# Two attention blocks on one core: where constants, weight permutations and key sums are made

## The chip, the cores and the metric

The kernel runs on one core of a Trainium2 chip. The metric is the time on the device in microseconds (us), from the first to the last instruction of the core, as a median of several executions. A profile is one execution taken apart by the hardware's profiler. Engines: PE is TensorE (matmuls), PEld its weight loads, DVE is VectorE, ACT is ScalarE, POOL is GpSimd, SP is SyncE, which here only issues DMA transfers. PSUM is the memory that matmuls write to, in eight banks; HBM is the main memory.

## The reference

Two independent blocks, A and B, share one program. Each has its own input of 2048 rows and 640 columns and its own weights.

```python
def _A_ref(x, wqkv, wo):                       # softmax attention, 32 heads of 20
    qkv = (x @ wqkv).reshape(B, S, 3, H, Dh) ...   # q, k, v
    scores = einsum("bhqd,bhkd->bhqk", q, k) * Dh ** -0.5
    p = softmax(scores, axis=-1)
    o = einsum("bhqk,bhkd->bhqd", p, v)
    return o.reshape(B, S, D) @ wo

def _B_ref(x, wqkv, wo):                       # linear attention, 32 heads of 20
    ...                                        # q, k, v as above
    phi = lambda t: where(t > 0, t + 1, exp(t)) + 1e-6
    pq, pk = phi(q), phi(k)
    kv = einsum("bhsd,bhse->bhde", pk, v)
    z = einsum("bhsd->bhd", pk)                # the key sums
    num = einsum("bhqd,bhde->bhqe", pq, kv)
    den = einsum("bhqd,bhd->bhq", pq, z)[..., None] + 1e-6
    return (num / den).reshape(B, S, D) @ wo

out = concatenate([_A_ref(A_x, A_wqkv, A_wo), _B_ref(B_x, B_wqkv, B_wo)], axis=-1)
# B, S, D, H = 1, 2048, 640, 32; everything bfloat16, values of about 0.05
```

## The kernel before

Block A is not computed with exponentials of all scores. The inputs keep every score small, so softmax is replaced by a second-order expansion, and a check at the end falls back to a general program if the bound doesn't hold. For each tile of 128 keys the kernel makes, per head, 242 features of the key (a one, the keys, their pairwise products) and sums feature times value over all keys. That is `t_T`, the product "ps<-f_big,f_Vp". A selection step (`sel` and `spread`, the tile `f_Tu`) lays these sums out for the queries. Queries are projected (`t_qj`), written to HBM, and loaded again in rearranged rows (`t_psi`, "f_big<-f_Qd"); VectorE forms their pairwise products, and `t_pv` multiplies them with the sums ("ps<-f_big,f_Tu"; such a unit has 48 matmuls). Block B projects keys and values, applies phi, sums key times value, and later does queries, denominators and the output.

All of it goes through one list of tasks. While the program is built, a small planner with assumed durations picks the order of tasks on each engine by priority; the hardware then runs each engine's list in order, with semaphores between them. `_C` holds the priorities. A smaller number goes first.

```python
_WS = 176
_C = dict(q=0.62, qs=0.04, ks=0.0, kd=0.02, bk=1.68, bks=0.0, bq=-2.52, bo=0.0, out=2.14, pv=0.0, fe=3.88,
          psi=5.12, r=-4.73, f=0.5, nm=3.12, op=6.09, kv=1.52, npo=0.16, bqs=0.05, bd=0.02, bn=4.94)
...
    def job(self, mms, cols, deps, prio=3.0, mode="pv", pool="aux", due=None):
        dur = sum(max(0.1, c / 2400.0 + 0.003) for c in cols)     # the planner's duration of a matmul job
...
```

Constants are made on the chip. `it` holds index patterns (iota), from which an identity, group masks (`M6`, `M32`), selections (`P`) and block masks (`mask`) are built. In the kernel before, the tasks form one chain, each depending on the one before it:

```python
    def mid_consts(self):
        ...
        last = self.event(1.5)
        ...
        def task(eng, dur, *ops):
            nonlocal last

            def fn(t):
                for f, r, w in ops:
                    sch.op(eng, f, reads=r, writes=w)
            last = plan.add(_Task(eng, dur, fn, prio=2.4), (last,))
        ...
        task("dve", 1.5,
             ...
                                        op=ALU.add), ("ident",), (K,)),
             (lambda e: e.tensor_copy(self.M32[:], m32), (K,), ("M32",)),
             (lambda e: e.memset(self.kvacc[:], 0.0), (), ("kva0",)),
             (lambda e: e.memset(self.mask, 0.0), (), ("mask0",)),
             (lambda e: e.memset(self.kvN[:], 0.0), (), ("kvN0",)))
        ops = [(lambda e: e.memset(self.GW[:], 0.0), (), ("GW",)),
               (lambda e: e.tensor_copy(self.GW[:, 8:14], self.M6[0:120, :]), ("M6",), ("GW",))]

        for x, (d, r) in enumerate(_SL):
            o = _off(d)[1]
            for a, n, b in ((0, 20 - r, o + r), (20 - r, r, o)):
                if n:
                    ops.append((lambda e, x=x, a=a, n=n, b=b: e.tensor_copy(
                        self.P[:, x, 6 * a:6 * (a + n)].rearrange("p (a h) -> p a h", h=6),
                        self.ident[0:123, b:b + n].unsqueeze(2).broadcast_to([123, n, 6])), ("ident",), ("P",)))
        ops.append((lambda e: e.tensor_copy(self.P[:, 0, 120:123], self.ident[0:123, 120:123]), ("ident",), ("P",)))
        task("pool", 9.0, *ops)
        m2 = scr[:, 0:168]
        for c in range(N_DC):
            h0, nh = self.hlo[c]
            w = 21 * nh
            task("pool", 0.6, (lambda e, h0=h0, nh=nh, c=c: e.iota(
                it[:, 0, 0:21 * nh], [[D_HEAD, nh], [0, 21]], base=D_HEAD * h0 - 128 * c, channel_multiplier=-1), (),
                ("it0",)))
            task("dve", 0.6,
                 (lambda e, w=w: e.tensor_scalar(m2[:, 0:w], it[:, 0, 0:w], 0.0, None, op0=ALU.is_le), ("it0",), (K,)),
                 (lambda e, c=c, w=w: e.scalar_tensor_tensor(self.mask[:, c, 0:w], it[:, 0, 0:w], -19.0, m2[:, 0:w],
                                                             op0=ALU.is_ge, op1=ALU.mult),
                  ("it0", K, "mask0"), (("mask", c),)))
        return last
```

Tiles of x are transposed by TensorE and copied out of PSUM by ScalarE or VectorE (`t_xt`, "f_xT<-ps"). Keys and values of tile t are projected in two halves of 320 columns. A key tile is copied out and copied twice more on ScalarE (`ext2`, `ext`), and then VectorE forms its products in two instructions, `even` and `odd`. The weights of the queries are put in another order by ScalarE after they have been loaded:

```python

        def perm(x, c):
            self.copy(x.eng, self.w[:, 0, c, 0:600].rearrange("p (b a h) -> p b a h", b=5, h=6),
                      self.w0r[:, c, 0:600].rearrange("p (b h a) -> p b a h", b=5, h=6), ("w0r",), (("w", 0, c),))
            self.copy(x.eng, self.w[:, 0, c, 600:640].rearrange("p (a h) -> p a h", h=2),
                      self.w0r[:, c, 600:640].rearrange("p (h a) -> p a h", h=2), ("w0r",), (("w", 0, c),))
        self.ew[0] = plan.add(_Task("none", 0.0, lambda t: None), [plan.add(_Task(
            "act", 0.9, lambda x, c=c: perm(x, c), prio=1.0), (e0,)) for c in range(N_DC)])
...
        def permB(x, c):
            self.copy(x.eng, self.wB[:, 0, c, :].rearrange("p (a h) -> p a h", h=N_HEADS),
                      self.w0B[:, c, :].rearrange("p (h a) -> p a h", a=D_HEAD), ("w0B",), (("wB", 0, c),))
        self.ewB[0] = plan.add(_Task("none", 0.0, lambda t: None), [plan.add(_Task(
            "act", 0.75, lambda x, c=c: permB(x, c), prio=2.2), (e1,)) for c in range(N_DC)])
```

The key sums of block B end as `zn[:, 0, :]`, 128 partitions by 5 numbers. They go to HBM and come back with another assignment of partitions:

```python

        def kvfin(_):
            zs = self.zs[:]
            sch.op("dve", lambda e: e.tensor_tensor(
                zs, self.kvacc[:].rearrange("p c (h j) -> p c h j", j=21)[:, :, :, 20],
                self.mask.rearrange("p c (h j) -> p c h j", j=21)[:, :, :, 20], op=ALU.mult),
                reads=tuple(("kva", c) for c in range(N_DC)) + tuple(("mask", c) for c in range(N_DC)), writes=("zs",))
            sch.op("dve", lambda e: e.tensor_reduce(self.zn[:, 0, :], zs, axis=AX.X, op=ALU.add), reads=("zs",),
                   writes=("zn0",))
            for c in range(N_DC):
        ...
        zd = self.Zd.ap()

        def small(e, dst, src):
            with self.nc.allow_non_contiguous_dma(reason="640 numbers in all"):
                return e.dma_start(dst, src)
        z1 = self.spd([lambda e: small(e, bass.AP(zd.tensor, zd.offset, [[1, 128], [128, N_DC], [1, 1]]), self.zn[:, 0, :])], (kvd,),
                      ("zn0",), ("Zd",), prio=0.4, lat=5.0)
        z2 = self.spd([lambda e: small(e, self.zn[:, 1, :], bass.AP(
            zd.tensor, zd.offset, [[1, 4], [D_HEAD, N_HEADS], [4, N_DC], [1, 1]]))], (z1,), ("Zd",), ("zn1",), prio=0.4, lat=5.0)
```

Of the kernel before, what the change touches and what calls it, by code (L numbers as in the profile page):

```python
# [6 lines left out]
F32 = mybir.dt.float32  # L7
BF16 = mybir.dt.bfloat16
I32 = mybir.dt.int32
AF = mybir.ActivationFunctionType  # L10
ALU = mybir.AluOpType
# [3 lines left out]
N_HEADS = 32  # L15
# [915 lines left out]
def _off(d):  # L931

    if d is None:
# [13 lines left out]
_C = dict(q=0.62, qs=0.04, ks=0.0, kd=0.02, bk=1.68, bks=0.0, bq=-2.52, bo=0.0, out=2.14, pv=0.0, fe=3.88,  # L947
          psi=5.12, r=-4.73, f=0.5, nm=3.12, op=6.09, kv=1.52, npo=0.16, bqs=0.05, bd=0.02, bn=4.94)


class _Fast:

    AUX = (4, 5, 6, 7)
    GB = 3
    NF = 2
# [28 lines left out]
    def alloc(self):  # L984
# [37 lines left out]
        self.zs = self.sb("f_zs", [128, N_DC, 8], F32)  # L1022
        self.zn = self.sb("f_zn", [128, 2, N_DC], F32)
# [27 lines left out]
        self.it = rb0[:, 0:360].bitcast(I32).rearrange("p (k n) -> p k n", k=2)  # L1051
# [52 lines left out]
    def fm(self, out, lhsT, rhs, start, stop, reads, writes, inc=True, sgc=False):  # L1104
        m = lhsT.shape[1]
        for j in range(0, m, 32):
            k = min(j + 32, m)
            self.sch.mm(out[j:k], lhsT[:, j:k], rhs, start=start, stop=stop, reads=reads, writes=writes, tp=(0, j),
                        inc=inc and k == m, sgc=sgc)
# [3 lines left out]
    def loads(self):  # L1113
# [44 lines left out]
        def perm(x, c):  # L1158
# [5 lines left out]
            "act", 0.9, lambda x, c=c: perm(x, c), prio=1.0), (e0,)) for c in range(N_DC)])  # L1164
# [6 lines left out]
        def permB(x, c):  # L1171
# [3 lines left out]
            "act", 0.75, lambda x, c=c: permB(x, c), prio=2.2), (e1,)) for c in range(N_DC)])  # L1175
# [14 lines left out]
    def consts(self):  # L1190
        sch, ps, it = self.sch, self.ps, self.it
        sch.op("dve", lambda e: e.memset(self.zt[:], 0.0), writes=("zt",))
        sch.op("pool", lambda e: e.iota(it[:, 0, 0:128], [[1, 128]], base=0, channel_multiplier=-1), writes=("it0",))
        sch.op("dve", lambda e: e.memset(self.warm[:], 0.0), writes=("warm",))
        sch.op("act", lambda e: e.activation(self.warm[:], self.warm[:], AF.Exp), writes=("warm",))
        sch.op("dve", lambda e: e.tensor_scalar(self.ident[:], it[:, 0, 0:128], 0.0, None, op0=ALU.is_equal),
# [11 lines left out]
    def mid_consts(self):  # L1208
        sch, it, rp, plan = self.sch, self.it, self.rp, self.plan
        scr = self.pqT[:, 0, :].bitcast(F32)  # L1210
        last = self.event(1.5)
        cl = (1.0 + _RNG * _RNG / 8.0) * float(D_HEAD) ** -0.5
        q = 0.5 / D_HEAD

        def task(eng, dur, *ops):
            nonlocal last

            def fn(t):
                for f, r, w in ops:
                    sch.op(eng, f, reads=r, writes=w)  # L1220
            last = plan.add(_Task(eng, dur, fn, prio=2.4), (last,))
        K = ("pqT", 0, 0)

        task("dve", 1.6,
             (lambda e: e.tensor_scalar(rp[:, 0:1], it[:, 0, 0:1], -1.0, None, op0=ALU.mult), ("it0",), ("rp",)),
# [9 lines left out]
        task("pool", 0.5,  # L1235
             (lambda e: e.iota(it[:, 1, 0:120], [[1, 6], [6, 20]], base=0, channel_multiplier=-1), (), ("it1",)))
        mf, e6, m32 = scr[0:120, 0:120], scr[0:120, 120:126], scr[:, 128:160]
        task("dve", 1.5,
             (lambda e: e.tensor_scalar(mf, it[0:120, 1, 0:120], 0.0, None, op0=ALU.is_equal), ("it1",), (K,)),
# [1026 lines left out]
```

## Time and profile before

| | before |
|---|---|
| median of 3 executions | 323.95 us (320.75 to 328.06) |
| span of the profiled execution | 324.1 us |
| mean granted TensorE clock | 0.974 of full speed |
| VectorE busy | 249.9 us |
| ScalarE busy | 190.8 us |
| HBM traffic over the span | 129 GB/s |

A row of the timeline gives the start, the length, the engine, the line of the kernel, the operation, what it writes and reads, its shape, a count, and in square brackets how long the engine was idle before it and what it waited for. A row of the wait list gives the waiting engine, line and tile, what released it, the total, the number of times and the longest. A row of a stretch gives its length and, for PE, PEld, DVE, ACT and POOL in this order, busy time and number of instructions; then the granted clock, the share of the DMA engines' time and the GB/s. Lines are those of the kernel before. Line 172 is the helper through which all matmuls go, so tiles tell them apart: "f_w,f_xT" are the key and value projections of block A, "f_wB,f_xB" those of block B, "f_xT,f_w" and "f_xB,f_wB" the query projections, "f_wo,f_w", and "f_pk" with "f_pq", "f_Vp" or "f_xB", the outputs.

### The profile page before, as it was taken

To read this page: it belongs to the slowest core of one execution; us is meant where nothing else is said; L and a number is where in the kernel's file an instruction comes from. 1 tells how busy PE (TensorE), PEld (TensorE's weight loads), DVE (VectorE), ACT (ScalarE), POOL (GpSimd) and SP (SyncE) were. 2 spreads that over 40 slices of the span, in tenths; PEclk is the share of its full clock that TensorE was granted. 3 is DMA by queue.
4 is the path that set the end of the run, shared out by engine and by line. 5 is a ranking of instruction groups with operands and counts; after the bars stand their busy time and mean duration, and the time that the engine had idled before them with its cause. 6 is when DMAs were issued, how large, how long until landed. Compare 5 with 4: busy or idle time off the path is not lost.

```text
span 324.1 us, 14979 instructions
## 1 busy us (share of the span) xinstructions
PE 289.9 (89%) x6866; PEld 203.3 (63%) x6866; DVE 249.9 (77%) x341; ACT 190.8 (59%) x390; POOL 10.0 (3%) x35
## 2 busy tenths in 40 slices
PE   6888959997999989998997969997988997999995
PEld 2566725886765645686884857665744453678874
DVE  6699964998959699897698794997978766996310
ACT  3678896987998713343344333547738365536653
POOL 2400000000000100000000000020000000000000
PEclk9799999999999978999799997999999999999999
DMA  8999756841013552736565363477588993534643
GB/s 257 276 198 172 113 88 170 292 110 38 4 34 110 155 161 70 179 72 153 141 175 137 98 174 110 99 201 174 70 215 219 236 203 103 156 120 149 171 169 104
DMA packets 59413, 47.60 MB, mean 147 GB/s; under 512 B 23645, under 2 KB 58265, under 8 KB 59345
## 3 DMA queue, kind: packets, MB, share of 16 engines
q1 hardware_dynamic: 53089, 38.60, 50.3%
q10 hardware_dynamic: 6256, 8.00, 9.2%
q8 instruction: 54, 0.88, 1.2%
q14 instruction: 14, 0.11, 0.2%
HBM read 30.65 MB, written 11.25 MB: 129 GB/s over the span
## 4 chain that ended last, share of the span: by engine, by line
PE 60%; DVE 14%; ACT 11%; DMA 7%; issue 5%; ACTq 1%; SPq 1%; POOL 0%; POOLq 0%; DVEq 0%
PE ps L172 60%; DMA f_Rc<-f_xT 3%; DVE f_big L1369 2%; DVE f_big L1364 2%; ACT f_w L1091 2%; DMA f_Nd<-f_Rc 2%; DMA f_big<-f_Qd 2%; ACT f_big L1091 2%; DVE f_Tu L1456 1%; ACT f_qk L1091 1%; ACT f_wB L1091 1%; ACT f_big L1345 1%; ACT f_Ks L1091 1%; DVE f_big L1601 1%; SPq L1589 1%
## 5 line engine op out<-in xcount | busy, mean ns | idle before, releaser
L1601 DVE TENSOR_TENSOR f_big<-f_big 120x1536 bf16<-120x1536 bf16 (+3 forms) x66 | 67.0, 1016 | 4.2 <-DMA f_big<-f_Qd 2.7
L172 PE MATMUL ps<-f_big,f_Tu 120*32 120x512 bf16 (+4 forms) x968 | 57.4, 373 | 6.0 <-issue 4.5
L172 PE MATMUL ps<-f_wB,f_xB 128*32 128x320 bf16 x1280 | 53.4, 309 | 2.5 <-issue 2.5
L172 PE MATMUL ps<-f_w,f_xT 128*32 128x320 bf16 x1280 | 48.8, 305 | 4.3 <-DVE f_xT L1095 3.0
L172 PEld LDWEIGHTS ps<-f_wB,f_xB 128*32 128x32 bf16 x1280 | 42.5, 100 | 8.8 <-issue 3.3
L172 PEld LDWEIGHTS ps<-f_big,f_Tu 120*32 120x32 bf16 (+2 forms) x968 | 31.5, 97 | 24.8 <-issue 6.2
L172 PEld LDWEIGHTS ps<-f_w,f_xT 128*32 128x32 bf16 x1280 | 34.8, 99 | 15.3 <-DVE f_xT L1095 3.2
L1091 ACT COPY f_xT<-ps 126x512 f32<-126x512 f32 (+3 forms) x33 | 16.8, 530 | 38.1 <-PE ps L172 35.0
L1369 DVE TENSOR_TENSOR f_big<-f_big 128x3200 bf16<-128x3200 bf16 x16 | 29.0, 1820 | 8.2 <-ACT f_big L1091 8.2
L1776 ACT ACTIVATE f_ex<-ps 128x320 f32<-128x320 f32 (+1 forms) x52 | 25.5, 500 | 16.5 <-PE ps L172 13.3
L1091 ACT CAST f_pk<-ps 128x320 bf16<-128x320 f32 (+3 forms) x64 | 25.5, 417 | 15.8 <-PE ps L172 12.7
L1364 DVE TENSOR_TENSOR f_big<-f_big,f_Ks 128x3200 bf16<-128x3200 bf16 x16 | 29.1, 1819 | 0.4 <-ACT f_Ks L1091 0.4
L172 PE MATMUL ps<-f_xT,f_w 128*32 128x512 bf16 (+2 forms) x440 | 27.2, 395 | 1.6 <-ACT f_w L1091 1.0
L172 PE MATMUL ps<-f_wo,f_w 128*32 128x320 bf16 x640 | 26.4, 300 | 0.3 <-ACT f_ex L1776 0.3
L1772 DVE TENSOR_SCALAR f_r<-ps 128x320 f32<-128x320 f32 x32 | 15.2, 486 | 12.5 <-ACT f_ex L1776 10.5
L172 PE MATMUL ps<-f_xB,f_wB 128*32 128x512 bf16 x400 | 23.9, 379 | 0.3 <-ACT f_ex L1776 0.3
L172 PEld LDWEIGHTS ps<-f_wo,f_w 128*32 128x32 bf16 x640 | 18.5, 97 | 5.6 <-ACT f_ex L1776 0.9
L1614 ACT ACTIVATE f_Dq<-f_big 120x512 bf16<-120x512 bf16 (+1 forms) x22 | 13.6, 619 | 13.7 <-DMA f_big<-f_Qd 11.2
L1091 ACT CAST f_qk<-ps 120x512 bf16<-120x512 f32 (+1 forms) x24 | 13.5, 586 | 12.0 <-PE ps L172 11.9
L172 PEld LDWEIGHTS ps<-f_xT,f_w 128*32 128x32 bf16 (+2 forms) x440 | 11.3, 98 | 14.5 <-ACT f_w L1091 2.0
L1091 ACT CAST f_big<-ps 128x320 bf16<-128x320 f32 (+1 forms) x33 | 14.3, 442 | 9.7 <-PE ps L172 9.3
L172 PE MATMUL ps<-f_big,f_Vp 128*32 128x242 bf16 x512 | 16.3, 267 | 3.5 <-DVE f_big L1364 3.1
(126 smaller groups left out, 369.4 us busy)
## 6 DMA issues: line engine op xcount, KB each, us to landing
f_big<-f_Qd SPq DMA_DIRECT2D x20, 480.0 KB, 5.1
f_big<-f_Qd SPq DMA_DIRECT2D x20, 240.0 KB, 6.1
f_Qd<-f_qk SPq DMA_DIRECT2D x20, 120.0 KB, 1.9
f_Rbc<-f_Nd ACTq DMA_DIRECT2D x3, 720.0 KB
f_w<-f_Nd ACTq DMA_DIRECT2D x4, 480.0 KB
out_dram<-f_pk SPq DMA_DIRECT2D x12, 160.0 KB, 3.6
f_wB<-in_B_wqkv_dram SPq DMA_DIRECT2D x2, 800.0 KB, 6.2
out_dram<-f_w SPq DMA_DIRECT2D x8, 160.0 KB, 5.4
```

The lines of the kernel that those rows point to most:

```text
L172: lambda e: e.matmul(out, lhsT, rhs, start=start, stop=stop, tile_position=tp, skip_group_check=sgc),
L1091: return self.sch.op("act", lambda e: e.copy(out, in_), reads=reads, writes=writes)
L1345: self.sch.op("act", lambda e: e.activation(F[:, :, 2:22], F[:, :, 222:242], AF.Square), reads=kk, writes=(("F", s, "d"),))
L1364: sch.op("dve", lambda e: e.tensor_tensor(F[:, :, 122:222].rearrange("p h (d a) -> p h d a", a=20), k0.unsqueeze(2).broadcast_to([128, 32, ...
L1369: sch.op("dve", lambda e: e.tensor_tensor(F[:, :, 22:122].rearrange("p h (d a) -> p h d a", a=20), k0.unsqueeze(2).broadcast_to([128, 32, ...
L1456: sch.op("dve", lambda e: e.tensor_tensor(dst.rearrange("p b (v h) -> p b v h", h=nh), src.rearrange("p b (h v) -> p b v h", h=nh), mask.u ...
L1589: fns = [lambda e: e.dma_start(sl[:, 0:4, :], self.q_load(u, 0, 4, 1)), lambda e: e.dma_start(sl[:, 9:11, :], self.q_load(u, 7, 2, 3))]
L1601: sch.op("dve", lambda e: e.tensor_tensor(sl[:, o:o + n, :], sl[:, a:a + 1, :].broadcast_to([120, n, N]), sl[:, b:b + n, :], op=ALU.mult), ...
L1614: sch.op("act", lambda e: e.activation(self.Dq[0:120, dq, 0:N], sl[:, 0, :], AF.Square), reads=(k0,), writes=(("Dq", dq),))
L1772: sch.op("dve", lambda e: e.tensor_scalar(r1, ps[:, j.bank, 0:n], 0.0, 1e-6, op0=ALU.max, op1=ALU.add), reads=(("ps", j.bank),), writes=(( ...
L1776: sch.op("act", lambda e: e.activation(ex, ps[:, j.bank, 0:n], AF.Exp), reads=(("ps", j.bank),), writes=(("ex", k, h),))
```

## The change

The change rebuilds how the constants are made. All six index patterns get room of their own, so that GpSimd can make them in one go and the chain falls apart into tasks that wait only for what they read; the aim is that constants are ready while the first loads land. Two clears (`kvacc`, `kvN`) go from VectorE to GpSimd, and the masks are built one after another without waiting for GpSimd in between. The permutations of query weights get a later priority and a longer assumed duration, so that they are placed between the copies of key tiles. The key sums are turned into five rows by a matmul with the identity, so that the store to HBM has long rows. Priorities and assumed durations are retuned all over, which changes the order of instructions on every engine. `TW` gives a name to the 32 columns of a matmul and leaves them as they are.

```diff
-_C = dict(q=0.62, qs=0.04, ks=0.0, kd=0.02, bk=1.68, bks=0.0, bq=-2.52, bo=0.0, out=2.14, pv=0.0, fe=3.88,
-          psi=5.12, r=-4.73, f=0.5, nm=3.12, op=6.09, kv=1.52, npo=0.16, bqs=0.05, bd=0.02, bn=4.94)
+_C = dict(q=0.62, qs=0.04, ks=0.0, kd=-0.005, bk=8.07, bks=0.0, bq=-3.62, bo=0.169, out=1.37, pv=0.0, fe=4.51,
+          psi=7.74, r=-3.6, f=-1.2, nm=0.91, op=4.0, kv=3.3, npo=0.1, bqs=0.0013, bd=0.0, bn=3.56)
...
         self.zs = self.sb("f_zs", [128, N_DC, 8], F32)
+        self.zb = self.sb("f_zb", [128, N_DC], BF16)
+        self.zr = self.sb("f_zr", [N_DC, 128], F32)
         self.zn = self.sb("f_zn", [128, 2, N_DC], F32)
...
-        self.it = rb0[:, 0:360].bitcast(I32).rearrange("p (k n) -> p k n", k=2)
+        self.it = rb0[:, 0:1096].bitcast(I32)
...
-            "act", 0.9, lambda x, c=c: perm(x, c), prio=1.0), (e0,)) for c in range(N_DC)])
+            "act", 1.45, lambda x, c=c: perm(x, c), prio=1.5), (e0,)) for c in range(N_DC)])
...
-            "act", 0.75, lambda x, c=c: permB(x, c), prio=2.2), (e1,)) for c in range(N_DC)])
+            "act", 1.3, lambda x, c=c: permB(x, c), prio=2.2), (e1,)) for c in range(N_DC)])
...
-        last = self.event(1.5)
         cl = (1.0 + _RNG * _RNG / 8.0) * float(D_HEAD) ** -0.5
         q = 0.5 / D_HEAD
-
-        def task(eng, dur, *ops):
-            nonlocal last
-
+        e0 = self.event(1.5)
+        ends = []
+
+        def task(eng, dur, deps, *ops):
             def fn(t):
                 for f, r, w in ops:
                     sch.op(eng, f, reads=r, writes=w)
-            last = plan.add(_Task(eng, dur, fn, prio=2.4), (last,))
-        K = ("pqT", 0, 0)
-
-        task("dve", 1.6,
-             (lambda e: e.tensor_scalar(rp[:, 0:1], it[:, 0, 0:1], -1.0, None, op0=ALU.mult), ("it0",), ("rp",)),
+            t = plan.add(_Task(eng, dur, fn, prio=2.4), [e0] + list(deps))
+            ends.append(t)
+            return t
+        K, i0, i1 = ("pqT", 0, 0), it[:, 0:128], it[0:120, 128:248]
+        im = [it[:, 256 + 168 * c:424 + 168 * c] for c in range(N_DC)]
+        ti = task("pool", 1.8, (),
+                  (lambda e: e.iota(i1, [[1, 6], [6, 20]], base=0, channel_multiplier=-1), (), ("it1",)),
+                  *[(lambda e, c=c: e.iota(im[c][:, 0:21 * self.hlo[c][1]], [[D_HEAD, self.hlo[c][1]], [0, 21]],
+                                           base=D_HEAD * self.hlo[c][0] - 128 * c, channel_multiplier=-1), (), (("itm", c),))
+                    for c in range(N_DC)])
+
...
-        task("pool", 0.5,
-             (lambda e: e.iota(it[:, 1, 0:120], [[1, 6], [6, 20]], base=0, channel_multiplier=-1), (), ("it1",)))
...
-             (lambda e: e.memset(self.kvacc[:], 0.0), (), ("kva0",)),
-             (lambda e: e.memset(self.mask, 0.0), (), ("mask0",)),
-             (lambda e: e.memset(self.kvN[:], 0.0), (), ("kvN0",)))
-        ops = [(lambda e: e.memset(self.GW[:], 0.0), (), ("GW",)),
-               (lambda e: e.tensor_copy(self.GW[:, 8:14], self.M6[0:120, :]), ("M6",), ("GW",))]
+        tm = task("dve", 1.4, (ti,),
...
-        task("pool", 9.0, *ops)
+        tp = task("pool", 6.0, (ti,), *ops)
+        task("pool", 2.5, (tm, tp),
+             (lambda e: e.memset(self.GW[:], 0.0), (), ("GW",)),
+             (lambda e: e.tensor_copy(self.GW[:, 8:14], self.M6[0:120, :]), ("M6",), ("GW",)),
+             (lambda e: e.memset(self.kvacc[:], 0.0), (), ("kva0",)),
+             (lambda e: e.memset(self.kvN[:], 0.0), (), ("kvN0",)))
         m2 = scr[:, 0:168]
+        prev = task("dve", 0.42, (tm,), (lambda e: e.memset(self.mask, 0.0), (), ("mask0",)))
         for c in range(N_DC):
-            h0, nh = self.hlo[c]
-            w = 21 * nh
-            task("pool", 0.6, (lambda e, h0=h0, nh=nh, c=c: e.iota(
-                it[:, 0, 0:21 * nh], [[D_HEAD, nh], [0, 21]], base=D_HEAD * h0 - 128 * c, channel_multiplier=-1), (),
-                ("it0",)))
-            task("dve", 0.6,
-                 (lambda e, w=w: e.tensor_scalar(m2[:, 0:w], it[:, 0, 0:w], 0.0, None, op0=ALU.is_le), ("it0",), (K,)),
-                 (lambda e, c=c, w=w: e.scalar_tensor_tensor(self.mask[:, c, 0:w], it[:, 0, 0:w], -19.0, m2[:, 0:w],
-                                                             op0=ALU.is_ge, op1=ALU.mult),
-                  ("it0", K, "mask0"), (("mask", c),)))
-        return last
+            w = 21 * self.hlo[c][1]
+            prev = task("dve", 0.6, (prev,),
+                        (lambda e, c=c, w=w: e.tensor_scalar(m2[:, 0:w], im[c][:, 0:w], 0.0, None, op0=ALU.is_le),
+                         (("itm", c),), (K,)),
+                        (lambda e, c=c, w=w: e.scalar_tensor_tensor(self.mask[:, c, 0:w], im[c][:, 0:w], -19.0, m2[:, 0:w],
+                                                                    op0=ALU.is_ge, op1=ALU.mult),
+                         (("itm", c), K, "mask0"), (("mask", c),)))
+        return plan.add(_Task("none", 0.0, lambda t: None), ends)
...
-        return self.job(mms, [240] * N_GRP, deps, prio=0.5, pool=None)
+        return self.job(mms, [293] * N_GRP, deps, prio=0.5, pool=None)
...
-                sch.barrier(("pool",), keys)
+                sch.barrier(("pool",), keys + ("kvN0", "kva0", "GW", "P"))
...
-                j = self.job(kvmm, [168] * (4 * len(cs)), ks + vs, prio=_C["kv"])
+                j = self.job(kvmm, [290] * (4 * len(cs)), ks + vs, prio=_C["kv"])
...
-                   writes=("zn0",))
+                   writes=("zn",))
+            sch.op("dve", lambda e: e.tensor_copy(self.zb[:], self.zn[:, 0, :]), reads=("zn",), writes=("zn0",))
...
-        z1 = self.spd([lambda e: small(e, bass.AP(zd.tensor, zd.offset, [[1, 128], [128, N_DC], [1, 1]]), self.zn[:, 0, :])], (kvd,),
-                      ("zn0",), ("Zd",), prio=0.4, lat=5.0)
+
+        def zmm(b):
+            sch.mm(ps[0:N_DC, b, 0:128], self.zb[:], self.ident[:], start=True, stop=True, reads=("zn0", "ident"),
+                   writes=(("ps", b),))
+            yield
+        zj = self.job(zmm, [128], (kvd,), prio=0.3, mode="full")
+
+        def zpost(x):
+            self.copy(x.eng, self.zr[:], ps[0:N_DC, zj.bank, 0:128], (("ps", zj.bank),), ("zr",))
+        zp = self.any(128, zpost, (zj,), prio=0.3, rel=(("aux", zj),))
+        z1 = self.spd([lambda e: e.dma_start(zd.rearrange("(c p) o -> c (p o)", p=128), self.zr[:])], (zp,),
+                      ("zr",), ("Zd",), prio=0.4, lat=4.0)
...
-        cj = self.job(cmm, [24] * 20, (zf,), prio=0.4)
+        cj = self.job(cmm, [24] * 3, (zf,), prio=0.4)
...
-                      tuple(("Mn", c, h) for c in range(N_DC) for h in range(2)), ("Md",), prio=0.4, lat=6.0)
+                      tuple(("Mn", c, h) for c in range(N_DC) for h in range(2)), ("Md",), prio=0.4, lat=8.0)
...
-            j = self.job(dmm, [512] * 5, qs + [zf], prio=_C["bd"])
+            j = self.job(dmm, [590] * 5, qs + [zf], prio=_C["bd"])
```

## The prediction

> **What bounds the kernel now.** I read the busy table first, then TensorE's waits, then the stretches where they fall. The busy table says that no engine is full, and TensorE is nearest to it:
>
> ```profile
> PE 289.9 (89%) x6866; PEld 203.3 (63%) x6866; DVE 249.9 (77%) x341; ACT 190.8 (59%) x390; POOL 10.0 (3%) x35
> ```
>
> Busy time of overlapping matmuls says little of how much work there is, so I counted the work at the rate the trace shows in crowded stretches. 600 matmuls of 128x320 took 20.85 us, so 34.8 ns each; 48 of 512 columns (one score-product unit) took 2.59 us, so 54 ns; 32 of 242 columns 0.85 us, so 26.5 ns. The terms: 3840 projections of 320 columns 133.6 us; 840 query projections of 512 columns 45.4; 21 full units and a short one 55.4; 512 of the key-feature sums 13.6; all else (key-value products 5.3, denominators 4.3, selection 4.9, warm-up 3.5, the rest about 10) 28. Sum 276 us. The span is 324, so 48 us are lost to waits, a low clock and the tail. Up to the first selection matmul at 112.4 us the count is 95.4 us, so 17 of the 48 fall before it and 31 after.
>
> The wait list of TensorE, whole kernel, the long ones (total us, times, longest):
>
> ```profile
> PE ps L172 <- issue: 9.6, 8, 2.4
> PE ps L172 <- DVE f_big L1364: 3.1, 2, 2.3
> PE ps L172 <- DVE f_xT L1095: 3.0, 1, 3.0
> PE ps L172 <- ACT f_pk L1091: 2.9, 3, 2.1
> PE ps L172 <- ACT f_ex L1776: 2.7, 3, 2.1
> ```
>
> Three of these the change touches. **First, the start.** The timeline at 7 us: VectorE clears three buffers before it copies out a transposed block of x, and TensorE stands for that copy:
>
> ```profile
> 7.20 0.76 DVE L1247 MEMSET f_kva<- 128x840 f32 x1
> 8.00 0.41 DVE L1248 MEMSET f_dn<- 128x420 uint32 x1
> 8.45 0.46 DVE L1249 MEMSET f_kvN<- 128x480 uint32 x1
> 8.83 0.23 DVE L1095 COPY f_xT<-ps 128x256 bf16<-128x256 bf16 x1
> 9.11 3.74 PE L172 MATMUL ps<-f_w,f_xT 128*32 128x320 bf16 x68 [2.99 <-DVE f_xT L1095]
> 12.17 1.83 DVE L1369 TENSOR_TENSOR f_big<-f_big 128x3200 bf16<-128x3200 bf16 x1 [3.12 <-ACT f_big L1091]
> ```
>
> The stretches around it show a second loss, the clock (third number from the right):
>
> ```profile
> 6.20:9.10 2.90, 0.00 (x0) 0.00 (x0) 2.54 (x10) 0.00 (x0) 2.14 (x9) 0.86 1.07 380
> 9.10:12.90 3.80, 3.79 (x70) 2.35 (x71) 0.73 (x1) 1.98 (x5) 2.73 (x12) 0.66 1.07 359
> ```
>
> 68 matmuls at 34.8 ns are 2.4 us; they took 3.4 (3.74 less one matmul's 0.3). **Second, ScalarE's block of weight permutations**, ten copies in one run, with the features of a key tile waiting behind it and TensorE behind those:
>
> ```profile
> 39.42 7.23 ACT L1091 COPY f_w<-f_Tu 128x600 bf16<-128x600 bf16 x10
> 43.49 1.01 PE L172 MATMUL ps<-f_big,f_Vp 128*32 128x242 bf16 x32 [2.33 <-DVE f_big L1364]
> 47.50 1.83 DVE L1369 TENSOR_TENSOR f_big<-f_big 128x3200 bf16<-128x3200 bf16 x1 [2.87 <-ACT f_big L1091]
> ```
>
> **Third, the key sums.** They go to HBM and back to change their layout. SyncE's own waits, then its timeline:
>
> ```profile
> SPq L1890 <- DMA f_Zd<-f_zn: 11.6, 1, 11.6
> 219.19 0.44 SPq L1890 DMA_DIRECT2D f_Zd<-f_zn  x1
> 231.20 0.61 SPq L1890 DMA_DIRECT2D f_zn<-f_Zd  x1
> 231.98 2.95 SPq L1589 DMA_DIRECT2D f_big<-f_Qd  x1
> 244.32 0.73 PE L172 MATMUL ps<-f_woB,f_pk 128*32 128x320 bf16 x16 [2.11 <-ACT f_ex L1776]
> ```
>
> SyncE stands 11.6 us for a store of 640 numbers, and the next query load, issued behind it, lands at about 241. ScalarE then stood 3.56 us and VectorE 1.70 for that load, and TensorE 2.11 for ScalarE.
>
> **What the Trainium skill says.** Perfetto Trace Analysis, Identifying the Most-Contended Engine: matmul busy share is no measure of how close TensorE is to its limit. The trace agrees: 290 us busy, 276 by the count. TensorE: Matmul & The Clock Gate, What's actually happening: an idle stretch lowers the array's clock until it has been busy again for some microseconds. The 0.86 and 0.66 around the first wait fit. DMA: Bandwidth & Descriptors, Rules for kernel authors: a non-contiguous last dimension becomes one descriptor per element. The old store is of that kind; the trace shows its 11.6 us. SBUF — State Buffer, SBUF: two separate sides: GpSimd and VectorE lock each other out of one shared port pair. Before, GpSimd's 17 selection copies took 5.30 us beside VectorE work (0.31 each), so I see no large delay of either.
>
> **The change, part by part.**
>
> *Start.* Two of the three clears go to GpSimd, the third goes behind the x copies, so these come at 7.1 instead of 8.83: 1.7 us less for TensorE. With a gap of 1.2 instead of 2.9 us the clock may hold: up to 1.0 more, of which I count 0.5. The five mask pairs (five of about 0.22 + 0.32, so 2.7 us) move from between the feature products, where VectorE was busy 9.86 of 10 us, into its 3.12 us hole. In VectorE's new order the first product stands behind the clear, the masks and three more x copies, so it begins near 11.5 instead of 12.17. Together VectorE is 2.8 us ahead: the 1.2 us of clears that went, plus the masks out of its full stretch, less what no longer fits in the hole.
>
> *GpSimd.* It makes six index patterns at once (0.25 to 0.29 each), then the selections (5.3 us), then the two clears. It is needed for nothing before 30 us and stays hidden.
>
> *Permutations.* The order shows one pair (1.26 + 0.22 us) at a time among the copies of later key tiles. The two TensorE gaps in this stretch, 2.33 and 1.02, should go: 3.3 us; VectorE's 2.87 too. The second set of permutations (6.9 us) now stands between the first query evictions: a hole of perhaps 2 us may remain there, as now around 94.
>
> *Order.* Before selection TensorE now does 29 halves of the second input's K/V projections instead of 15, and fewer query projections: 104.3 us of counted work instead of 95.4. VectorE does 99.2 instead of 91.6 by the same kind of count. VectorE started selection at 112.9, 21.3 us behind its count. Taking off 2.8 and 2.9 and 1 for a smaller query burst leaves 14.6: 113.8. TensorE was 17.0 behind; less 1.7, 0.5 and 3.3 that is 11.5: 115.8. So selection begins near 115, and what remains after it is 171.9 us of work instead of 180.7.
>
> *Key sums.* A one-column-tile transpose, one eviction and a store of five 512-byte rows replace 640 separate numbers. I estimate the store at 2 us, from the query stores of the page (1.9). The later load is also ordered behind two query loads. The 2.11 us wait and 0.3 beside it should go: 2.4. New cost: one matmul, one eviction of about 0.3 us on ScalarE, one cast of 0.2 on VectorE, all beside other work.
>
> *Sum.* 1.7 + 0.5 + 3.3 + 2.4 = 7.9 us. As a check: 115 + 171.9 + (31 - 2.4) = 315.5. I take 315.5.
>
> **The rivals.**
>
> A: *The waits only move.* The plan that orders instructions was retuned all over, and new priorities may put TensorE behind VectorE or a PSUM bank elsewhere. For it: VectorE's early work rises by 7.6 us, and queries come late, with 13 projections in the last four tiles. Against it: VectorE ends 15 us before TensorE now and has room. Then the time stays at 320 to 325.
>
> B: *Only the start and permutations count.* The late query load might be hidden if a deeper cause holds TensorE near 244, such as PSUM banks held by exponentials. For it: ScalarE is named, not the load. Then about 318.
>
> C: *The retuned order is worth more than its parts*, since the second half lost 31 us of which I claim 2.4. Gaps of 2.12 at 152.6, 1.30 at 270 and 0.86 at 275 are all waits that other orders can fill. Then 309 to 312. The unexplained waits ("issue", 9.6 us) I leave as they are: instruction counts don't change.
>
> **Range and chances.** The centre is 315.5. The spread of the time before is 320.75 to 328.06, so single runs move by 1%; A and C lie some 5 us to either side. Range 309 to 322. Faster by over 2% means under 317.5, a bit above the centre: 0.60. Within 2%: 0.36. Slower: 0.04, since no part adds work to the bounding engine.
>
> **What would show it.** TensorE's first wait at 1 to 1.3 us instead of 2.99, with the clock above 0.66 after it. No VectorE or TensorE gap over 1 us behind permutation copies. Selection begins between 113 and 118. The store of key sums lands in under 4 us and no query load is issued late behind it. Wrong, if selection begins after 119, if the late part still takes over 205 us from there, or if waits on ScalarE evictions grow by as much as these shrink.

## The result: faster, but not by the sum of the parts

The changed kernel takes 311.19 us (median, 310.15 to 316.57) against 324.35 (320.75 to 328.06) in the same comparison: ratio 0.962, 95% interval 0.951 to 0.973. The profiled executions span 308.6 and 324.1 us.

The busy table of the changed kernel shows nearly the same work in a shorter span; every engine is within 4 us of what it was:

```profile
PE 286.1 (93%) x6867; PEld 200.9 (65%) x6867; DVE 252.6 (82%) x345; ACT 188.5 (61%) x386; POOL 11.5 (4%) x37
```

So time was lost less often. Its TensorE waits (total us, times, longest):

```profile
PE ps L172 <- issue: 8.4, 7, 1.9
PE ps L172 <- DVE f_xT L1098: 1.8, 1, 1.8
PE ps L1295 <- DVE f_xT L1098: 1.4, 1, 1.4
PE ps L172 <- ACT f_pk L1094: 1.1, 3, 0.5
PE ps L172 <- ACT f_ex L1784: 0.7, 1, 0.7
```

The waits for key features (3.1) are down to 0.6, those for ScalarE's f_pk and f_ex from 5.6 to 1.8; one of 1.4 is new. If I add up all waits in TensorE's timeline after the first 5 us, they come to 28.6 us before and 16.7 after: 11.6 to 7.3 ahead of the first selection matmul, 17.0 to 9.4 behind it. That is 11.9 of the 15.5 us between the spans. The other 3.6 are not waits; the mean granted clock rose from 0.974 to 0.980, which at 0.6% of the span is, by estimate, about 2 of them.

**The start**, timeline of the changed kernel (VectorE, GpSimd, TensorE):

```profile
7.08 0.48 DVE L1098 COPY f_xT<-ps 128x256 bf16<-128x256 bf16 x2
7.41 2.90 PE L172 MATMUL ps<-f_w,f_xT 128*32 128x320 bf16 x80 [1.76 <-DVE f_xT L1098]
7.92 0.17 DVE L1277 TENSOR_SCALAR f_pq<-f_Rbc 128x147 f32<-128x147 int32 x1
8.47 1.72 DVE L1277 TENSOR_SCALAR f_pq<-f_Rbc 128x147 f32<-128x147 int32 x1
8.47 0.80 POOL L1270 MEMSET f_kva<- 128x840 f32 x1
9.20 0.90 POOL L1271 MEMSET f_kvN<- 128x960 bf16 x1
12.69 0.28 PE L1295 MATMUL ps<-f_id,f_pk 128*128 128x128 bf16 x2 [1.42 <-DVE f_xT L1098]
12.94 1.82 DVE L1377 TENSOR_TENSOR f_big<-f_big 128x3200 bf16<-128x3200 bf16 x1
```

The copies of x come at 7.08 instead of 8.83. But the same selection test takes 0.17 us at 7.92 and 1.72 at 8.47, as long as GpSimd's two clears beside it. The later copies of x and the first feature product stand behind it: TensorE gets a new wait of 1.42, and the product starts at 12.94, later than the 12.17 of before.

**The permutations** come one pair at a time, and TensorE hardly waits behind them (timeline):

```profile
42.95 1.58 ACT L1094 COPY f_w<-f_Tu 128x600 bf16<-128x600 bf16 x2
50.94 1.01 PE L172 MATMUL ps<-f_big,f_Vp 128*32 128x242 bf16 x32 [0.19 <-DVE f_big L1372]
54.37 1.57 ACT L1094 COPY f_w<-f_Tu 128x600 bf16<-128x600 bf16 x2
```

**The key sums**: made on VectorE at 200.60, stored, loaded again, and multiplied out into f_kvZ (timeline; SyncE, then VectorE):

```profile
200.60 0.20 DVE L1882 TENSOR_REDUCE f_zn<-f_zs 128x5 f32<-128x40 f32 x1
206.05 0.26 SPq L1910 DMA_DIRECT2D f_Zd<-f_zr  x1
210.99 0.61 SPq L1899 DMA_DIRECT2D f_zn<-f_Zd  x1
217.97 0.32 DVE L1916 TENSOR_TENSOR f_kvZ<-f_zn,f_M 128x160 bf16<-128x160 f32 x1
```

The store has landed within 4.9 us of its issue: the load that needs it goes out then, behind a pair of query loads. The changed kernel with the old priorities (below) bounds it closer, since there SyncE issues nothing in between and waits for the store:

```profile
223.11 0.26 SPq L1910 DMA_DIRECT2D f_Zd<-f_zr  x1
224.29 0.61 SPq L1899 DMA_DIRECT2D f_zn<-f_Zd  x1
```

There it has landed within 1.2 us. Selection begins at 116.96; from there it takes 191.6 us (before: 211.7).

### The profile page after: what moved, and what is told of

Its sections match the earlier page's. It is cut to its first block, busy times and chain, and to the rows that moved or that the text cites. A ratio compares the mean times of both kernels' runs of the same rounds, so it can differ in the third digit from the quotient of the medians.

```text
span 308.6 us, 14979 instructions
## 1 busy us (share of the span) xinstructions
PE 286.1 (93%) x6867; PEld 200.9 (65%) x6867; DVE 252.6 (82%) x345; ACT 188.5 (61%) x386; POOL 11.5 (4%) x37
## 4 chain that ended last, share of the span: by engine, by line
PE 66%; DVE 17%; ACT 6%; DMA 5%; issue 4%; ACTq 1%; POOL 0%; DVEq 0%; POOLq 0%
PE ps L172 66%; DMA f_Rc<-f_xT 3%; DVE f_big L1609 3%; DMA f_Nd<-f_Rc 2%; DVE f_Tu L1464 2%; DVE f_big L1372 2%; DVE f_big L1377 2%; ACT f_ex L1784 1%; DVE f_r L1780 1%; ACT f_pk L1094 1%; DVE f_pq L1277 1%; ACT f_big L1094 1%; DVE f_pk L1803 1%; DVE f_dn L2029 1%; ACT f_xT L1094 1%
## 5 line engine op out<-in xcount | busy, mean ns | idle before, releaser
L172 PE MATMUL ps<-f_big,f_Tu 120*32 120x512 bf16 (+5 forms) x968 | 57.6, 373 | 2.5 <-issue 1.9
L172 PE MATMUL ps<-f_wB,f_xB 128*32 128x320 bf16 x1280 | 49.5, 299 | 4.1 <-issue 2.8
L172 PEld LDWEIGHTS ps<-f_big,f_Tu 120*32 120x32 bf16 (+3 forms) x968 | 32.1, 96 | 21.1 <-issue 2.8
L172 PEld LDWEIGHTS ps<-f_wB,f_xB 128*32 128x32 bf16 x1280 | 37.1, 97 | 12.8 <-issue 3.5
L1094 ACT COPY f_xT<-ps 126x512 f32<-126x512 f32 (+3 forms) x29 | 15.5, 539 | 37.5 <-PE ps L172 33.4
L1094 ACT CAST f_pk<-ps 128x320 bf16<-128x320 f32 (+4 forms) x63 | 25.5, 415 | 13.9 <-PE ps L172 12.9
L172 PE MATMUL ps<-f_xB,f_wB 128*32 128x512 bf16 x400 | 25.4, 379 | 0.1
L172 PE MATMUL ps<-f_big,f_Vp 128*32 128x242 bf16 x512 | 16.7, 267 | 3.1 <-issue 2.5
L172 PEld LDWEIGHTS ps<-f_xT,f_w 128*32 128x32 bf16 (+2 forms) x440 | 12.0, 99 | 11.6 <-issue 2.1
L172 PEld LDWEIGHTS ps<-f_xB,f_wB 128*32 128x32 bf16 x400 | 13.2, 96 | 8.9 <-ACT f_ex L1784 0.3
L1094 ACT CAST f_big<-ps 128x320 bf16<-128x320 f32 (+1 forms) x31 | 13.5, 436 | 7.7 <-PE ps L172 7.3
```

The costliest lines, as they stand in the source:

```text
L172: lambda e: e.matmul(out, lhsT, rhs, start=start, stop=stop, tile_position=tp, skip_group_check=sgc),
L1094: return self.sch.op("act", lambda e: e.copy(out, in_), reads=reads, writes=writes)
```

## The experiments

The theory of the prediction is a sum: each part is worth the wait it removes. Its rival C says that the order of instructions, dealt anew by the planner, carries the gain. The traces cannot part them, since all changed at once. Two kinds of run can. Some take one part out of the changed kernel or put one alone into the kernel before, and the planner then deals a new order. Others change one thing and keep every engine's order.

**Store as a column, order kept.**

```diff
-        z1 = self.spd([lambda e: e.dma_start(zd.rearrange("(c p) o -> c (p o)", p=128), self.zr[:])], (zp,),
-                      ("zr",), ("Zd",), prio=0.4, lat=4.0)
+        z1 = self.spd([lambda e: small(e, bass.AP(zd.tensor, zd.offset, [[1, 128], [128, N_DC], [1, 1]]),
+                                       self.zn[:, 0, :])], (zp,), ("zr", "zn"), ("Zd",), prio=0.4, lat=4.0)
```

> The changed kernel with every engine's order kept, but the key sums stored as the old column of 4-byte pieces (128x5x1) where the row store (5x128) stood; the small product and the copy that make the row stay. The sums' own theory: the store takes some 11 us instead of under 5, SyncE's later query load is issued that much later, and TensorE waits for it again: 312 to 315 us. The order theory: the changed order has moved the queries that hung on it, so the late store costs under 1 us: 308 to 310 us.

Measured: 321.93 us, ratio to before 0.997 (0.992 to 1.001); span 319.5, 10.9 more than the changed kernel. The timeline (SyncE, VectorE, TensorE) shows where:

```profile
208.16 0.40 SPq L1899 DMA_DIRECT2D f_Zd<-f_zn  x1
218.21 0.61 SPq L1899 DMA_DIRECT2D f_zn<-f_Zd  x1
226.20 1.80 PE L172 MATMUL ps<-f_big,f_Tu 120*32 120x512 bf16 x20 [2.15 <-issue]
231.29 0.33 DVE L1916 TENSOR_TENSOR f_kvZ<-f_zn,f_M 128x160 bf16<-128x160 f32 x1 [8.92 <-DMA f_zn<-f_Zd]
231.67 1.25 PE L172 MATMUL ps<-f_pq,f_kvZ 128*32 128x512 bf16 x5 [1.23 <-DVE f_kvZ L1916]
235.24 4.88 PE L172 MATMUL ps<-f_big,f_Tu 123*32 123x512 bf16 x44 [2.32 <-DVE f_big L1609]
```

The load is issued 10 us after the store, and VectorE stands 8.92 us for it, with the query products of `t_psi` behind in its list. TensorE then waits, and its clock falls: 44 matmuls take 4.88 us where the changed kernel needs 2.56. Both theories missed the size (312 to 315 and 308 to 310) and the way: not a late query load but VectorE's place in its own order is what costs. The column store is only part of it: the load back takes 13.1 us here (218.21 to 231.29), at most 7.0 in the changed kernel (210.99 to 217.97). With those 7.0, by estimate, VectorE would have stood some 3 us; why the load was slower no run shows. Before, the row of f_kvZ was here:

```profile
235.84 0.33 DVE L1897 TENSOR_TENSOR f_kvZ<-f_zn,f_M 128x160 bf16<-128x160 f32 x1
```

That is 17 us behind its sums (218.63), without a wait: the old order hid the slow store from VectorE. The Trainium skill (PSUM — Partial Sum Buffer, Engine vs sequencer instructions) calls VectorE's queue a strict FIFO; the 8.92 us agree.

**Permutations in one block, order kept.** All five pairs of a set run where the first stood:

```diff
+        def block(x, k, f):                    # k: "A" or "B", once each
+            if first[k]:
+                first[k] = False
+                for c in range(N_DC):
+                    f(x, c)
-            "act", 1.45, lambda x, c=c: perm(x, c), prio=1.5), (e0,)) for c in range(N_DC)])
+            "act", 1.45, lambda x, c=c: block(x, "A", perm), prio=1.5), (e0,)) for c in range(N_DC)])
```

and the same for the second set.

> The changed kernel with every other engine's order kept, but all five weight-row pairs of a set copied by ScalarE where the first pair stood, and nothing at the four later places (both sets): one block of some 7.2 us and one of some 7 us, as before the change. My theory: TensorE gaps of 1 to 2.4 us come back after the first block and VectorE waits for ScalarE; first selection matmul 2 to 3.5 us later than in the changed kernel (117 to 118.5 us), time 313 to 315 us. Rival, that ScalarE has the slack and only the re-dealt order counted: under 1 us.

Measured: 323.76 us, ratio 0.993 (0.990 to 0.997); span 318.6. Timeline (ScalarE, VectorE, TensorE):

```profile
42.99 7.21 ACT L1094 COPY f_w<-f_Tu 128x600 bf16<-128x600 bf16 x10
50.56 0.89 DVE L1787 TENSOR_SCALAR f_r<-ps 128x320 f32<-128x320 f32 x2 [5.62 <-ACT f_ex L1791]
50.90 4.45 PE L172 MATMUL ps<-f_w,f_xT 128*32 128x320 bf16 x80 [4.58 <-ACT f_big L1094]
88.99 6.35 ACT L1094 COPY f_wB<-f_Tu 128x640 bf16<-128x640 bf16 x5
95.87 2.32 PE L172 MATMUL ps<-f_xT,f_w 128*32 128x512 bf16 x20 [4.02 <-ACT f_qk L1094]
```

Two waits of 4.58 and 4.02 and the clock after them (80 matmuls in 4.45 us instead of 2.9, 20 in 2.32 instead of some 1.1): 11.3 us together. Selection begins at 128.5, 11.6 later; the part from there takes 190.1 us, as in the changed kernel. So in this order spreading the pairs is worth three times the 3.3 I gave it; the 313 to 315 us expected of this run were too low as well.

**The clears on GpSimd.** Two runs. The first gave the clears a planned time of 40 us:

```diff
-             (lambda e: e.memset(self.kvacc[:], 0.0), (), ("kva0",)),
-             (lambda e: e.memset(self.kvN[:], 0.0), (), ("kvN0",)))
+        task("pool", 1.7, (self.event(40.0),),
+             (lambda e: e.memset(self.kvacc[:], 0.0), (), ("kva0",)),
+             (lambda e: e.memset(self.kvN[:], 0.0), (), ("kvN0",)))
```

> The changed kernel with GpSimd's two large clears (kvacc, kvN) moved to about 40 us; all else keeps its order. Port theory: VectorE's selection test at 8.47 us lasts 0.2 us instead of 1.72, TensorE's wait of 1.42 us at 12.69 goes, the first feature product starts near 11.5 us instead of 12.94, and another VectorE operation near 40 us is drawn out by up to 1.7 us; time 307 to 310 us. Rival, that the 1.72 us comes from something else (the integer operand, the masks' own chain): the operation stays long and nothing changes by more than 0.3 us.

Measured: 312.21 us, 0.960 (0.955 to 0.966). A miss in its design: the planner's time sets only the order, nothing makes GpSimd wait, and the clears ran at 8.45 as ever. It is the changed kernel a second time (the test took 1.71), and the measure for the runs beside it.

The second makes the clears read the masks, which is a true dependence:

```diff
+        mk = tuple(("mask", c) for c in range(N_DC))
+        task("pool", 1.7, (prev,),
+             (lambda e: e.memset(self.kvacc[:], 0.0), mk, ("kva0",)),
+             (lambda e: e.memset(self.kvN[:], 0.0), mk, ("kvN0",)))
```

> The changed kernel with GpSimd's two large clears made to wait for the last mask. Shared-port theory: the selection test at 8.47 us lasts 0.25 us instead of 1.72, the last mask comes 1.5 us sooner, near 10.9 us; then the clears (1.7 us) run from there and the VectorE operation beside them, a copy of x or the first feature product, is drawn out instead if it too shares the ports; if that kind does not, the first product starts near 11.5 us. Time 309 to 312 us. Rival (the long selection test has another cause): it stays at 1.7 us and the clears merely come later.

Measured: 314.24 us, 0.963 (0.958 to 0.969): no difference from the changed kernel that can be told. Timeline (VectorE, GpSimd):

```profile
8.46 0.24 DVE L1275 TENSOR_SCALAR f_pq<-f_Rbc 128x147 f32<-128x147 int32 x1
11.01 0.80 POOL L1282 MEMSET f_kva<- 128x840 f32 x1 [2.49 <-DVE f_dn L1277]
11.74 0.90 POOL L1283 MEMSET f_kvN<- 128x960 bf16 x1
12.08 0.51 DVE L1098 COPY f_xT<-ps 128x256 bf16<-128x256 bf16 x2 [1.14 <-PE ps L1297]
13.04 1.82 DVE L1379 TENSOR_TENSOR f_big<-f_big 128x3200 bf16<-128x3200 bf16 x1
```

The test falls from 1.71 to 0.24 us, so the clears were its cause. The two copies from PSUM beside the second clear take 0.25 us each, as without a clear beside them (0.48 for the two at 7.08): they are not held up. The first product still starts at 13.04, because in this execution TensorE's first 80 matmuls ran at a lower clock (4.42 us instead of 2.90) and the transposes came late; what the 1.4 us are worth by themselves stays open.

**Old priorities and durations in the changed kernel.** `_C` and the five assumed durations as before the change, the rest new:

```diff
-_C = dict(q=0.62, qs=0.04, ks=0.0, kd=-0.005, bk=8.07, ...
+_C = dict(q=0.62, qs=0.04, ks=0.0, kd=0.02, bk=1.68, ...
-        return self.job(mms, [293] * N_GRP, deps, prio=0.5, pool=None)
+        return self.job(mms, [240] * N_GRP, deps, prio=0.5, pool=None)
```

> The changed kernel with all old priorities and assumed durations of the order planner (permutations excepted), so with the moved constants, spread permutations and the key-sum row only. My theory (the four named places carry it): 311 to 316 us. Order theory: the 8.8 us that the second half gained beyond the key sums go, and the part after the first selection matmul takes over 198 us again instead of 191.6: 316 to 320 us.

Measured: 316.32 us (315.18 to 318.57), 0.974 (0.967 to 0.980), 4 us above the repeat of the changed kernel in the same comparison (311.72 to 314.09). It is what the order theory expected (316 to 320 us, over 198 us after the first selection matmul: 201.6), and 0.3 us above the range of mine. Yet it also lies near the sum of my prediction: three parts, 315.5. The next runs show that this is no support for the sum.

**The permutations as before in the changed kernel** (old assumed durations and priority, the planner deals anew):

```diff
-            "act", 1.45, lambda x, c=c: perm(x, c), prio=1.5), (e0,)) for c in range(N_DC)])
+            "act", 0.9, lambda x, c=c: perm(x, c), prio=1.0), (e0,)) for c in range(N_DC)])
```

> The changed kernel with the weight permutations back at their old assumed durations (0.9 and 0.75 us) and priority 1.0, so that they stand in blocks again. My theory (spreading them was worth 3.3 us of TensorE): TensorE gaps of 1 to 2.3 us come back between 35 and 60 us, the first selection matmul starts 2 to 4 us later than 117.0, and the time is 311 to 313 us. Order theory: the first half is not where the gain came from, and the time stays within 2 us of 309 us, up or down, by what the new order does later.

Measured: 332.47 us, 1.023 (1.017 to 1.030), some 20 us above both theories. Selection begins at 123.3 instead of 117.0, but most is lost late. TensorE stands at block B's output projections (timeline):

```profile
298.01 7.27 PE L172 MATMUL ps<-f_pk,f_pq 128*32 128x320 bf16 x160 [10.50 <-DVE f_pq L2047]
```

In the changed kernel the main run of the same product has no wait and comes with other work still at hand:

```profile
265.49 6.00 PE L172 MATMUL ps<-f_pk,f_pq 128*32 128x320 bf16 x153
271.32 2.89 PE L172 MATMUL ps<-f_wo,f_w 128*32 128x320 bf16 x80
```

**The constants as before in the changed kernel** (`consts`, `mid_consts`, `it` and the barrier's keys from the kernel before):

```diff
-        self.it = rb0[:, 0:1096].bitcast(I32)
+        self.it = rb0[:, 0:360].bitcast(I32).rearrange("p (k n) -> p k n", k=2)
-        e0 = self.event(1.5)
+        last = self.event(1.5)
```

> The changed kernel with the old constants part alone: index patterns one by one between masks, clears on VectorE before the copies of x. Sum theory: 2 us slower than the changed kernel, 312 to 315 us. Order theory: the planner, given other tasks at the start, deals an order for which the priorities were not tuned, and the loss is 5 us or more, 316 us and up, most of it after the first selection matmul.

Measured: 336.37 us, 1.036 (1.030 to 1.042), as the order theory expected. It starts selection at 118.0, 1 us from the changed kernel; the rest is lost behind it, in the same chain (timeline):

```profile
283.12 0.32 DVE L1912 TENSOR_TENSOR f_kvZ<-f_zn,f_M 128x160 bf16<-128x160 f32 x1 [5.37 <-DMA f_zn<-f_Zd]
302.45 7.58 PE L172 MATMUL ps<-f_pk,f_pq 128*32 128x320 bf16 x160 [8.68 <-DVE f_pq L2043]
```

**One part alone in the kernel before.** The new priorities and durations:

```diff
-_C = dict(q=0.62, qs=0.04, ks=0.0, kd=0.02, bk=1.68, ...
+_C = dict(q=0.62, qs=0.04, ks=0.0, kd=-0.005, bk=8.07, ...
```

> The kernel before with the new priorities and assumed durations of the planner alone; constants, permutations and key sums as before. Order theory (the new order carries half of the gain by itself): 317 to 320 us. Rival (the order needs the quick key sums and the spread permutations, for which it was tuned): no gain or a loss, 322 to 332 us, with VectorE waiting for the key sums.

Measured: 343.59 us, 1.055 (1.049 to 1.062), far worse than either theory. Timeline (GpSimd, VectorE, TensorE):

```profile
11.97 1.83 DVE L1369 TENSOR_TENSOR f_big<-f_big 128x3200 bf16<-128x3200 bf16 x1 [2.73 <-ACT f_big L1091]
12.02 1.83 POOL L1260 COPY f_pq<-f_id 123x3 bf16<-123x3 bf16 x1
276.22 0.33 DVE L1897 TENSOR_TENSOR f_kvZ<-f_zn,f_M 128x160 bf16<-128x160 f32 x1 [5.71 <-DMA f_zn<-f_Zd]
306.55 7.33 PE L172 MATMUL ps<-f_pk,f_pq 128*32 128x320 bf16 x160 [10.68 <-DVE f_pq L2028]
```

The key-sum row:

```diff
-        z1 = self.spd([lambda e: small(e, bass.AP(zd.tensor, ...), self.zn[:, 0, :])], (kvd,), ("zn0",), ...
+        z1 = self.spd([lambda e: e.dma_start(zd.rearrange("(c p) o -> c (p o)", p=128), self.zr[:])], (zp,), ("zr",), ...
```

> The kernel before with the key-sum row alone (small product, copy, 5x128 store); the planner deals the order anew with the old priorities. My theory of the sum: 2.4 us faster, 321 to 323 us. What the column-store run of the changed kernel showed (10.7 us, most of it VectorE waiting for the key sums at its next place in the order) lets another hold: the old order left some 17 us between the sums and their use, so that VectorE never waited for them, and the row alone is worth under 3 us; it is worth its 10 us only with an order that uses the sums early.

Measured: 328.04 us, 1.004 (0.999 to 1.008): nothing, which fits the second view and not the sum.

The permutations:

```diff
-            "act", 0.9, lambda x, c=c: perm(x, c), prio=1.0), (e0,)) for c in range(N_DC)])
+            "act", 1.45, lambda x, c=c: perm(x, c), prio=1.5), (e0,)) for c in range(N_DC)])
```

> The kernel before with the weight permutations' new assumed durations and priority alone (old priorities, constants and key sums otherwise). Sum theory (each part is worth what it removes, wherever it stands): 3.3 us faster, near 321 us, with the blocks of 7.2 us on ScalarE and the TensorE gaps of 2.33 and 1.02 us after them gone. Order theory (the parts only pay together): within 2 us of before, either way, or slower.

Measured: 329.31 us, 1.012 (1.006 to 1.017), slower. The TensorE gap of 2.33 is gone, as is the block, and TensorE's waits ahead of selection fall from 11.6 to 9.9 us. Behind it they grow from 17.0 to 20.4, and VectorE waits 4.76 us for the key sums at 247.99. So the gap went where the part stands, and more was lost later.

The permutations and the key-sum row (both edits above):

> The kernel before with the spread permutations and the key-sum row, old priorities, old constants: the changed kernel with old priorities (316.3 us) less its new constants. Sum theory: 3.3 + 2.4 us faster than before, 318 to 320 us, and 2.2 us above the 316.3 us. Order theory: no telling from the parts; anything from 314 to 330 us, and the difference is to be found in the waits after 150 us, not where the parts stand.

Measured: 334.89 us, 1.032 (1.026 to 1.037). By the sum it should have been 319, and it lies above the order theory's 330 too. With the constants added it is the run at 316.32: they take 18.6 us off here.

The constants, patterns, masks and clears:

```diff
-        self.it = rb0[:, 0:360].bitcast(I32).rearrange("p (k n) -> p k n", k=2)
+        self.it = rb0[:, 0:1096].bitcast(I32)
-        last = self.event(1.5)
+        e0 = self.event(1.5)
```

> The kernel before with the moved index patterns, masks and selections alone. Sum theory: 2.2 us faster, 321 to 323 us, with the copies of x at 7.1 us and the first product under 12 us but for the selection test drawn out by GpSimd's clears (1.7 us), which may take 1 us of it. Order theory: within 2 us of before or slower.

Measured: 332.66 us, 1.026 (1.020 to 1.032), although the copies of x came at 7.19 as planned. Here the same constants add 8 us.

All runs together, sorted by when the key sums are made. Waits are all those in TensorE's timeline after 5 us; the last column is its wait for VectorE's division at B's output projections, where the profile names that. (For the row alone the median counts disturbed executions, which the ratio leaves out; its profile was of such a one and is not in the table.)

| kernel | ratio to before | key sums made, us | span, us | TensorE waits, us | of it at B's output |
|---|---|---|---|---|---|
| changed | 0.962 | 200.6 | 308.6 | 16.7 | 0 |
| changed, column store | 0.997 | 202.7 | 319.5 | 22.8 | 0 |
| changed, repeat | 0.960 | 204.2 | 310.5 | 19.2 | 0 |
| changed, clears after masks | 0.963 | 204.4 | 312.6 | 19.5 | 0 |
| changed, one block | 0.993 | 211.7 | 318.6 | 25.6 | 0 |
| changed, old priorities | 0.974 | 216.2 | 313.3 | 20.9 | 1.9 |
| before | 1 | 218.6 | 324.1 | 28.6 | 0.9 |
| before, permutations | 1.012 | 224.4 | 327.2 | 30.3 | 2.0 |
| before, permutations and row | 1.032 | 225.3 | 331.4 | 33.6 | 6.7 |
| before, constants | 1.026 | 227.6 | 328.9 | 30.7 | 3.3 |
| changed, old permutations | 1.023 | 250.9 | 331.0 | 37.2 | 10.5 |
| before, new priorities | 1.055 | 252.7 | 339.7 | 43.0 | 10.7 |
| changed, old constants | 1.036 | 269.3 | 333.9 | 36.0 | 8.7 |

Span less waits is 291 to 298 us in every row: the orders differ mostly in waits (16.7 to 43.0). By and large the orders that make the key sums late end late. In the three latest TensorE has run out of other work when B's last outputs are divided, 9 to 11 us of it. That this lateness is the cause in the middle rows too is argued from the ranking, not shown.

What makes the sums late in these three can be read in TensorE's timeline. The last key-value products of block B are two jobs, of 48 and 32 matmuls. In the changed kernel (first row) they stand together; with the old permutations (second and third row) the order puts 34 us of other work between them, and the late row has no wait before it:

```profile
191.95 1.71 PE L172 MATMUL ps<-f_pk 128*32 128x147 bf16 x80
203.69 0.98 PE L172 MATMUL ps<-f_pk 128*32 128x147 bf16 x48
238.30 0.70 PE L172 MATMUL ps<-f_pk 128*32 128x147 bf16 x32
```

With the new priorities in the kernel before the small job stands at 240.7 in the same way; with the old constants both come late, at 257.6 and 267.3. So the planner's place for one job of 0.7 us holds up the whole chain in two of the three. No run moved that job alone.

## Why the prediction came out, and where it failed

The time, 311.2 for 315.5, lies in the range. The step that failed is the sum, "1.7 + 0.5 + 3.3 + 2.4 = 7.9 us": no term of it keeps its value from one order to another. Three of the four waits it names are gone in the trace, and the first is shorter; yet of the parts alone none makes the kernel before faster (1.004, 1.012, 1.026). Taking one out of the changed kernel costs most of the gain with the order held (permutations 0.993, key sums 0.997), and with the order dealt anew from a third of it (the priorities) to more than all of it (permutations or constants). Term by term:

- *Start, 1.7 + 0.5.* The wait fell from 2.99 to 1.76, 1.2 us (I had said to 1 to 1.3), and 1.42 came back at 12.69: on balance nothing. "First product near 11.5": 12.94. "I see no large delay of either": wrong. I read the shared ports from GpSimd's selection copies, 0.31 us from one to the next, but half of these ran while VectorE stood idle (9.1 to 12.2 us), and the clears I moved there are 0.80 and 0.90. The clock is no term to count on: it held here (80 matmuls in 2.90 us) and did not in the repeat (4.22).
- *Permutations, 3.3.* The mechanism is right, blocks stop TensorE. The size depends on the order: 10 to 12 us in the new one, where two waits of over 4 us return; with the old priorities, dealt anew, waits ahead of selection fell by 1.7 us and the time did not fall. What spreading is worth with the old order held was not measured. The hole of 2 us that I feared behind the second set did not come.
- *Selection near 115.* 116.96, inside the 113 to 118. Loss ahead of it fell from 17.0 to 12.7; I had said 10.7.
- *Key sums, 2.4.* The store did land in time: within 4.9 us here, within 1.2 with the old priorities. But the chain by which I sized it, a late query load and ScalarE, is not what the store can cost: in the new order it is VectorE waiting 8.92 us in its list, 10.9 us of span, for a store and a load back that are both slower. With the old priorities, dealt anew, the whole part is worth nothing.
- *After selection, 171.9 + 28.6.* 191.6 instead of 200.5: the 9 us that rival C spoke of.

C has the number (309 to 312), but not as it stands either: the new order alone makes the kernel before 5.5% slower. What is shown is that no part alone, and not the new priorities alone, makes the kernel before faster, while the three parts without the new priorities bring 2.6 of the 3.8%. The old priorities with all three parts cost 4 us over the changed kernel; the same priorities with two of them, some 23 us. That the three with the old priorities came to 316.3, within 1 us of my 315.5, I take for chance: two of the same terms gave 334.9 where I expected 319. A and B fall: the waits did not only move, and in the new order the row store is not without effect.

One rival is untested: how far the time moves when the planner deals anew and no part changes, after a small change of one priority, say. Without that, no run with a new deal can tell what it owes to its part and what to the deal; those with the order held can.

## What to carry to other kernels

Where a planner deals the order of all engines, a part's worth is measured with the order held; parts tried one by one with the order dealt anew gave losses of 0 to 5.5% here for a set that gains 3.8% together. To size a slow transfer, look not only at who waits for it now but at how soon the new order wants the result: 17 us of distance hid a 12 us store, and the order that gains needs the result early. A chain that ends in the last outputs (key sums, denominators, division) belongs early in every list, while TensorE still has other work: three runs here waited 9 to 11 us at its end. That an earlier place alone cures this was not tested.

## What was not expected of the hardware

- *GpSimd clears stop a VectorE operation.* A selection test of 0.17 to 0.25 us took 1.71 to 1.72 beside clears of 0.80 and 0.90 and waited for both. The reverse is in the new-priorities run above: a GpSimd copy of 123x3 took 1.83 us, the length of VectorE's product beside it, where the changed kernel shows 0.36. The Trainium skill (SBUF — State Buffer, SBUF: two separate sides) says that whoever starts first holds the shared pair for the whole instruction and the other blocks fully. Of VectorE it says this for operations in a two-port mode, and for those with two inputs in SBUF against a GpSimd instruction that reads SBUF. Both cases agree, if the test ran in such a mode, which no run shows; the copies from PSUM, 0.25 us beside a clear, fit its dedicated pair.
- *The slow clock after a wait costs a third of it or as much again.* Behind the 4.58 us wait 80 matmuls took 4.45 us instead of 2.90, at a granted clock of 0.64; behind 2.32 us, 44 took 4.88 instead of 2.56, at 0.50. The Trainium skill (TensorE: Matmul & The Clock Gate, What's actually happening) describes such a loss after idling; these clocks agree.
- *Waits that nothing explains.* TensorE stands 4 to 12 us in all in stops of up to 2.7 us marked "issue", at other places in each order; only the run with the old constants had almost none (0.2). Their cause stays open.
